# Lightning attention and a gated FFN on one core: state decay products one block ahead on POOL, crossbar transposes ahead of the output stores on SP

## Chip, core and metric

One core of a Trainium2 chip. The metric is device time in microseconds (us): the median of several executions of the same program. A profile is one further execution, recorded instruction by instruction. Engine names: PE is TensorE, DVE is VectorE, ACT is ScalarE, POOL is GpSimd; SP issues DMAs. POOL issues DMAs too.

## What is computed

Four sequences of 768 positions with eight heads of 64 (q, k, v), a decay `lam` per head, then a feed-forward layer on the 3072 x 512 result with a sigmoid gate and 1536 hidden features. The reference goes through the sequence in blocks and carries a state per head:

```
intra = (q_b k_b^T * Dmask) v_b              # Dmask[i,j] = lam^(i-j) for i >= j, else 0
inter = (q_b * lam^(pos+1)) kv_state
out_b = intra + inter
kv_state = lam^block * kv_state + (k_b * lam^(block-1-pos))^T v_b
...
y = (sigmoid(x w_gate) * (x w_val)) w_out    # x: out, as 3072 x 512
```

## The kernel before

The kernel takes blocks of 128 positions, so it has six blocks, 0 to 5, each over all four sequences (512 tokens). Matmul inputs are bf16. The heads are kept in pairs, so one 128 x 128 matmul tile holds two heads of 64.

Per block n there are these pieces; the line numbers are those of the profile of the kernel before.

- `load`: q, k, v of the block by three DMAs that POOL issues (L78, tiles qb, kb, vb; four buffers each). They convert fp32 to bf16 on the way, in packets of one head's row.
- `transpose_by_dma` (blocks 2 to 5): two crossbar transposes that SP issues (L151), first Q into QR, then K into KR. Blocks 0 and 1 are transposed on PE (L160, L169, L184, L190).
- `piece_t`: QS = QR times the powers of lam, on DVE (L177), once for each half of the sequences (two of the four).
- `piece_s`: scores sp, on PE (L206) from KR and QS. `piece_m`: MT = sp times the mask, on DVE (L214).
- `piece_a`: the attention output op, on PE from the state Sb and QS (L220) and from V and MT (L227); ACT copies it to XT (L234).
- `make_kd`: kd = K times a decay, one POOL product over 128 x 2048 (L238), two buffers.
- `piece_c`: the new state. PE makes cp from kd and V (L246). POOL makes sd = Sb times the block's decay, one product for each of the four sequences (L251, four buffers), and DVE adds the two into Sb (L259). The matmuls of the next block and the next sd read Sb.
- `piece_gv`: for one of 12 groups of 128 hidden features the gate gp (L270) and the value vp (L276), the sigmoid sg on ACT (L273) and ht = sg times vp on DVE (L279). `piece_gvh` is the same for half of the tokens.
- `piece_po`: the output po for one sequence of the block, 12 matmuls on PE (L302), a copy to ob on ACT (L305, four buffers), and a store that SP issues (L306).

PSUM has two pools: five tiles for attention (tags tq, tk, sp, op, cp) and three for the feed-forward part (gp, vp, po), given out in turn. So a gate or value matmul group waits until the ht or sg that read the tile three places earlier is through.

The order of each engine's instructions is the order in which they are written, for all of PE, POOL, DVE, ACT and SP; nothing is reordered. An engine that waits holds up everything behind it, and so does a DMA queue: SP's stores and transposes go in their written order, and so do POOL's loads and products.

In the order of before, `fetch(n)` writes the load, kd and the two transposes of a block together. `fetch(2)` stands in the middle of block 0's end, and `fetch(n+1)` at the head of block n's loop for n = 2, 3, 4. On POOL this gives, from the end of the weight loads: kd(1), load 2, kd(2), sd of block 1, load 3, kd(3), sd of block 2, load 4, kd(4), sd of block 3, load 5, kd(5), sd of block 4. On SP: the transposes of block 2, eight stores (blocks 0 and 1), transposes of block 3, four stores, transposes of block 4, four stores, transposes of block 5, eight stores.

A block of the loop (n = 2, 3, 4) runs on PE as: gate and value groups 0 and 1 with the state pieces between and behind them, groups 2 and 3 each followed by a half of QS for block n+1 (on DVE), group 4, scores of the first half, groups 5, 6, 7, scores of the second half, group 8, attention output of the first half, groups 9 to 11, attention output of the second half, then the four outputs po of block n.

Of the kernel before, what the change touches and what calls it, by code (L numbers as in the profile page):

```python
# [8 lines left out]
FP32 = mybir.dt.float32  # L9
BF16 = mybir.dt.bfloat16  # L10
AF = mybir.ActivationFunctionType
ALU = mybir.AluOpType
# [4 lines left out]
def kernel(  # L17
# [11 lines left out]
    nc = tc.nc  # L29

    B, H, S, D = q.shape
    C = 128
    NSTEP = S // C
    HP = H // 2
# [8 lines left out]
    qkv = ctx.enter_context(tc.tile_pool(name="qkv", bufs=4))  # L43
    kdp = ctx.enter_context(tc.tile_pool(name="kdp", bufs=2))
# [26 lines left out]
    def load(n, what, b0, b1):  # L71
        sl = slice(n * C, (n + 1) * C)
        for c in what:
            lst, src = {"q": (Q, q), "k": (K, k), "v": (V, v)}[c]
            if n not in lst:
                lst[n] = qkv.tile([128, B, H, D], BF16, tag=c + "b", name=c + "b")
            t = lst[n]
            nc.gpsimd.dma_start(  # L78
                out=t[:, b0:b1],
                in_=src[b0:b1, :, sl, :].rearrange("b h s d -> s (b h) d"))  # L80
# [6 lines left out]
    def load_wo(i, w):  # L87
        fs = slice(i * w, (i + 1) * w)
        nc.gpsimd.dma_start(out=WO[:, fs, :], in_=wo_r[:, fs, :])
# [35 lines left out]
    for hp in range(HP):  # L125
# [3 lines left out]
    dec = const.tile([128, HP], FP32, tag="dec")  # L129
# [4 lines left out]
                            in1=pk.rearrange("p (g u) -> p u g", u=2).unsqueeze(3).to_broadcast([128, 2, HP, C]),  # L134
                            op=ALU.mult)
# [11 lines left out]
    def transpose_by_dma(n):  # L147
        QR[n] = trsb.tile([128, B, HP, C], BF16, tag="QR", name="QR", bufs=2)
        kt = trsb.tile([128, B, HP, C], BF16, tag="KR", name="KR", bufs=2)
        for dst, src in ((QR[n], Q[n]), (kt, K[n])):  # L150
            nc.sync.dma_start_transpose(out=dst.rearrange("p b g c -> p (b g) c"),  # L151
                                        in_=src.rearrange("p b h d -> p (b h d)"))
        for bp in range(2):
            KS[n, bp] = kt[:, 2 * bp:2 * bp + 2]
# [39 lines left out]
    Sb = stp.tile([128, B, HP, 128], BF16, tag="Sb", name="Sb")  # L194
# [16 lines left out]
    def piece_m(n, b):  # L211
        MT[n, b] = mtp.tile([128, 2, HP, C], BF16, tag="MT", name="MT")
        for u in range(2):
            nc.vector.tensor_tensor(out=MT[n, b][:, u], in0=SP[n, b][u], in1=mask[:, u], op=ALU.mult)  # L214

    def piece_a(n, bs):
        for b in bs:
            OP[n, b] = ps_at.tile([128, HP, C], FP32, name="op", tag="ps")
            for hp in range(HP if n > 0 else 0):
                nc.tensor.matmul(OP[n, b][:, hp, :], lhsT=Sb[:, b, hp, :],  # L220
                                 rhs=QS[n, b // 2][:, b % 2, hp, :],
                                 start=(hp == 0), stop=False, skip_group_check=True)
        for b in bs:
            for hp in range(HP):
                for u in range(2):
                    us = slice(u * 64, (u + 1) * 64)
                    nc.tensor.matmul(OP[n, b][us, hp, :], lhsT=V[n][:, b, 2 * hp + u, :],  # L227
                                     rhs=MT[n, b][:, u, hp, :],
                                     start=(n == 0 and hp == 0), stop=(hp == HP - 1),
                                     skip_group_check=True)  # L230
        if n not in XT:
            XT[n] = xtp.tile([128, NMT, B, C], BF16, tag="XT", name="XT")
        for b in bs:
            nc.scalar.copy(XT[n][:, :, b, :], OP[n, b])  # L234

    def make_kd(n):
        KD[n] = kdp.tile([128, B, H, D], BF16, tag="kd", name="kd")
        nc.gpsimd.tensor_tensor(  # L238
            out=KD[n], in0=K[n],
            in1=kds.unsqueeze(1).unsqueeze(3).to_broadcast([128, B, H, D]), op=ALU.mult)  # L240

    def piece_c(n, bs):
        for b in bs:
            cp = ps_at.tile([128, HP, 128], FP32, name="cp", tag="ps")
            for hp in range(HP):
                nc.tensor.matmul(cp[:, hp, :], lhsT=KD[n][:, b, 2 * hp:2 * hp + 2, :],  # L246
                                 rhs=V[n][:, b, 2 * hp:2 * hp + 2, :],
                                 start=(hp == 0), stop=(hp == HP - 1), skip_group_check=True)
            if n > 0:
                sd = kdp.tile([128, HP, 128], FP32, tag="sd", name="sd", bufs=4)  # L250
                nc.gpsimd.tensor_tensor(out=sd, in0=Sb[:, b],  # L251
                                        in1=dec.unsqueeze(2).to_broadcast([128, HP, 128]),
                                        op=ALU.mult)
            for u in range(2):
                us = slice(u * 64, (u + 1) * 64)
                if n == 0:
                    nc.vector.tensor_copy(Sb[us, b, :, us], cp[us, :, us])
                else:
                    nc.vector.tensor_tensor(out=Sb[us, b, :, us], in0=cp[us, :, us],  # L259
                                            in1=sd[us, :, us], op=ALU.add)  # L260
# [4 lines left out]
    def piece_gv(n, ft):  # L265
        fs = slice(ft * 128, (ft + 1) * 128)
        x = XT[n].rearrange("p m b c -> p m (b c)")
        gp = ps_ff.tile([128, TCH], FP32, name="gp", tag="ff")
        for mt in range(NMT):
            nc.tensor.matmul(gp, lhsT=WG[:, mt, fs], rhs=x[:, mt, :],  # L270
                             start=(mt == 0), stop=(mt == NMT - 1))
        sg = htp.tile([128, TCH], BF16, tag="sg", name="sg", bufs=3)
        nc.scalar.activation(sg, gp, AF.Sigmoid)  # L273
        vp = ps_ff.tile([128, TCH], FP32, name="vp", tag="ff")
        for mt in range(NMT):
            nc.tensor.matmul(vp, lhsT=WV[:, mt, fs], rhs=x[:, mt, :],  # L276
                             start=(mt == 0), stop=(mt == NMT - 1))
        HT[n, ft] = htp.tile([128, TCH], BF16, tag="ht", name="ht", bufs=2 * NFT)
        nc.vector.tensor_mul(HT[n, ft], sg, vp)  # L279
# [19 lines left out]
    def piece_po(n, tt):  # L299
        po = ps_ff.tile([128, DM], FP32, name="po", tag="ff")  # L300
        for ft in range(NFT):
            nc.tensor.matmul(po, lhsT=HT[n, ft][:, tt * 128:(tt + 1) * 128],  # L302
                             rhs=WO[:, ft, :], start=(ft == 0), stop=(ft == NFT - 1))
        ob = osb.tile([128, DM], FP32, tag="ob", name="ob")
        nc.scalar.copy(ob, po)  # L305
        nc.sync.dma_start(out=out[tt * S + n * C:tt * S + (n + 1) * C, :], in_=ob)  # L306
# [12 lines left out]
    load(1, "v", 2, 4)  # L319
    for i in range(3):  # L320
        load_wo(i, NFT // 3)
    make_kd(1)

    idle(10)
    piece_tq0(0)
# [23 lines left out]
    def c(n, bp):  # L349
        piece_c(n, [2 * bp, 2 * bp + 1])  # L350

    def t(n, bp):
        piece_t(n, bp)

    def sc(n, bp):
        piece_s(n, [2 * bp, 2 * bp + 1])
        piece_m(n, 2 * bp)

    def m(n, bp):
        piece_m(n, 2 * bp + 1)  # L360

    def a(n, bp):
        piece_a(n, [2 * bp, 2 * bp + 1])

    def fetch(n):
        load(n, "qkv", 0, B)
        make_kd(n)
        transpose_by_dma(n)

    def gv(n, *fts):  # L370
        for ft in fts:
            piece_gv(n, ft)

    def gvh(n, i, *fts):
        for ft in fts:
            piece_gvh(n, ft, i)
# [2 lines left out]
    c(0, 0)  # L379
    gv(0, 4)  # L380
    c(0, 1)
    gv(0, 5, 6, 7)
    t(1, 0)
    gv(0, 8)
# [4 lines left out]
    a(1, 0)  # L389
    gv(0, 11)  # L390
    t(1, 1)
    fetch(2)
    gvh(1, 0, 0, 1)
    sc(1, 1)
    gvh(1, 0, 2)
# [6 lines left out]
    c(1, 0)  # L402
    gv(1, 9)
    c(1, 1)
    gv(1, 10, 11)
    piece_po(0, 0)
    t(2, 0)
# [5 lines left out]
    sc(2, 1)  # L413
    m(2, 1)
    piece_po(0, 3)
    piece_po(1, 0)
    a(2, 0)
    piece_po(1, 1)
# [3 lines left out]
    for n in range(2, NSTEP):  # L422
        nx = n + 1
        if nx < NSTEP:
            fetch(nx)
            gv(n, 0)
            c(n, 0)
            gv(n, 1)
            c(n, 1)
            gv(n, 2)  # L430
            t(nx, 0)
            gv(n, 3)
            t(nx, 1)
            gv(n, 4)
            sc(nx, 0)
            gv(n, 5)
            m(nx, 0)
            gv(n, 6, 7)
            sc(nx, 1)
            gv(n, 8)  # L440
            m(nx, 1)
            a(nx, 0)
            gv(n, 9, 10, 11)
            a(nx, 1)
        else:
            gv(n, *range(NFT))
        for tt in range(B):
            piece_po(n, tt)
# [30 lines left out]
```

## Time and profile before

| what | value |
|---|---|
| median of 4 runs (lowest, highest) | 243.15 us (242.41, 244.54) |
| profiled execution: its own time, and its span | 243.9 us, 241.7 us |
| PE busy in the span | 225.1 us (93%) |
| DVE, ACT, POOL busy | 105.6, 80.1, 85.0 us |
| mean granted TensorE clock | 0.985 |
| kd on POOL | 6 products, 3.6 us each |
| sd on POOL | 16 products, 1.09 us each |
| one load of q, k or v (blocks 2 to 5), issue to landing | 8.0, 10.3, 13.0 us (medians) |
| a transpose QR or KR, issue to landing | 7.8 or 6.2 us (medians) |

The span goes from the first to the last instruction; the own time has 2.2 us around it. A row of a timeline reads: start, duration, engine, line, operation, output<-inputs, shape, count, and in brackets the idle time before it with what ended it. SPq and POOLq are the instructions by which SP and POOL issue DMAs. In the DMA counts, q0 is the queue of the loads that POOL issues and q1 that of the stores and transposes that SP issues: packets, MB, and the time of the packets as a share of 16 engines.

### The profile page before, as it was taken

What the parts mean: (1) busy time and instruction counts of PE and PEld (TensorE: products, weight loads), DVE (VectorE), ACT (ScalarE), POOL (GpSimd) and SP (SyncE); (2) the same over time, 40 slices, a digit from 0 to 9 for tenths busy, and PEclk for the clock granted to TensorE, in tenths of its full rate; (3) what the DMA queues carried; (4) which work ended last, traced back from release to release, by engine and by line L of the source; (5) the groups of instructions that cost most, each with busy time, mean ns of one, the idle gap of its engine ahead of it and who ended that gap; (6) DMA issues with size and microseconds to landing.
All of it is one profiled execution on the core that took longest, in us unless ns stands there. A gap on an engine that the chain in (4) does not pass through costs nothing.

```text
span 241.7 us, 3816 instructions
## 1 busy us (share of the span) xinstructions
PE 225.1 (93%) x1528; PEld 116.0 (48%) x1553; DVE 105.6 (44%) x184; ACT 80.1 (33%) x145; POOL 85.0 (35%) x70
## 2 busy tenths in 40 slices
PE   7789999999999999829999999999999999999993
PEld 2444555886534555314554444554544554444441
DVE  2373855843738004455630298720397620243300
ACT  5453234453211332202431332332222432333221
POOL 8999650934962980991000085000000000000000
PEclk9999999999999999967999999999999999999999
DMA  9999999999999899999902480002560002200022
GB/s 58 137 182 195 174 183 169 206 155 157 136 112 200 169 94 180 160 155 156 81 3 87 122 140 3 0 3 87 148 115 1 0 3 87 87 0 0 3 87 87
DMA packets 102289, 24.89 MB, mean 103 GB/s; under 512 B 91520, under 2 KB 99200, under 8 KB 102272
## 3 DMA queue, kind: packets, MB, share of 16 engines
q0 software_dynamic: 82032, 14.16, 77.7%
q1 hardware_dynamic: 20240, 10.49, 19.5%
q8 instruction: 12, 0.20, 0.3%
q14 instruction: 5, 0.04, 0.0%
HBM read 28.32 MB, written 6.29 MB: 143 GB/s over the span
## 4 chain that ended last, share of the span: by engine, by line
PE 84%; DMA 6%; SPq 2%; DVE 2%; issue 2%; ACT 2%; POOL 0%; POOLq 0%; ACTq 0%; DVEq 0%
PE po L302 25%; PE vp L276 22%; PE gp L270 22%; DMA KR<-kb 4%; PE sp L206 3%; PE vp L293 3%; PE op L227 3%; DMA kb<-in_k_dram 3%; PE gp L287 2%; SPq L151 2%; PE op L220 2%; DVE MT L214 2%; PE cp L246 2%; PE tk L169 1%; ACT KS L172 0%
## 5 line engine op out<-in xcount | busy, mean ns | idle before, releaser
L279 DVE TENSOR_TENSOR ht<-sg,vp 128x512 bf16<-128x512 bf16 x65 | 44.5, 686 | 94.5 <-PE vp L276 93.2
L270 PE MATMUL gp<-XT,WG 128*128 128x512 bf16 x249 | 66.1, 383 | 1.0 <-issue 0.5
L276 PE MATMUL vp<-XT,WV 128*128 128x512 bf16 x255 | 66.8, 383 | 0.3
L273 ACT ACTIVATE sg<-gp 128x512 bf16<-128x512 f32 x65 | 38.8, 597 | 81.7 <-PE gp L270 77.6
L302 PE MATMUL po<-WO,ht 128*128 128x512 bf16 x281 | 63.3, 379 | 0.9 <-DVE ht L279 0.5
L302 PEld LDWEIGHTS <-ht 128*128 128x128 bf16 x288 | 27.6, 98 | 33.7 <-issue 0.8
L238 POOL TENSOR_TENSOR kd<-kb,kds 128x2048 bf16<-128x2048 bf16 x6 | 21.8, 3632 | 58.8 <-PE cp L246 30.2
L276 PEld LDWEIGHTS <-WV 128*128 128x128 bf16 x260 | 25.7, 99 | 31.3 <-issue 1.1
L270 PEld LDWEIGHTS <-WG 128*128 128x128 bf16 x260 | 24.2, 98 | 27.7 <-issue 2.1
L214 DVE TENSOR_TENSOR MT<-sp,mask 128x512 bf16<-128x512 f32 x48 | 30.5, 682 | 8.1 <-PE sp L206 8.1
L305 ACT COPY ob<-po 128x512 f32<-128x512 f32 x24 | 14.1, 586 | 51.4 <-PE po L302 47.7
L251 POOL TENSOR_TENSOR sd<-Sb,dec 128x512 f32<-128x512 bf16 x16 | 17.0, 1086 | 0.0
L234 ACT CAST XT<-op 128x512 bf16<-128x512 f32 x24 | 13.0, 588 | 9.9 <-PE op L227 9.8
L259 DVE TENSOR_TENSOR Sb<-cp,sd 64x256 bf16<-64x256 f32 x32 | 13.4, 420 | 1.9 <-POOL sd L251 1.0
L78 POOL DMA_DIRECT2D qb<-in_q_dram x8 | 11.9, 1484 | 1.0 <-POOLq L463 0.8
L78 POOL DMA_DIRECT2D kb<-in_k_dram x8 | 11.5, 1433 | 1.1 <-DMA qb<-in_q_dram 1.1
L78 POOL DMA_DIRECT2D vb<-in_v_dram x8 | 11.4, 1430 | 0.8 <-DMA WG<-in_moe_w_gate_dram 0.6
L206 PE MATMUL sp<-QS,KR 64*128 64x128 bf16 x128 | 5.4, 229 | 6.2 <-DMA KR<-kb 5.8
L140 PE MATMUL wm<-zero 128*128 128x512 bf16 x23 | 8.2, 489 | 1.5 <-DVE zero L97 1.2
L177 DVE TENSOR_TENSOR QS<-QR,lamq 128x1024 bf16<-128x1024 bf16 x8 | 6.4, 796 | 6.2 <-DMA QR<-qb 6.2
L206 PEld LDWEIGHTS <-KR 64*128 64x128 bf16 x128 | 3.9, 99 | 9.6 <-DMA KR<-kb 6.3
L293 PE MATMUL vp<-XT,WV 128*128 128x256 bf16 x56 | 8.4, 272 | 0.1
(51 smaller groups left out, 114.7 us busy)
## 6 DMA issues: line engine op xcount, KB each, us to landing
out_dram<-ob SPq DMA_DIRECT2D x24, 256.0 KB, 2.0
qb<-in_q_dram POOLq DMA_DIRECT2D x4, 512.0 KB, 8.0
kb<-in_k_dram POOLq DMA_DIRECT2D x4, 512.0 KB, 10.3
vb<-in_v_dram POOLq DMA_DIRECT2D x4, 512.0 KB, 13.0
WG<-in_moe_w_gate_dram POOLq DMA_DIRECT2D x6, 256.0 KB, 9.5
WV<-in_moe_w_val_dram POOLq DMA_DIRECT2D x6, 256.0 KB, 9.8
WO<-in_moe_w_out_dram POOLq DMA_DIRECT2D x3, 512.0 KB, 15.2
qb<-in_q_dram POOLq DMA_DIRECT2D x4, 256.0 KB, 7.5
```

The source lines that it names most:

```text
L78: nc.gpsimd.dma_start(out=t[:, b0:b1], in_=src[b0:b1, :, sl, :].rearrange("b h s d -> s (b h) d"))
L206: nc.tensor.matmul(sp[u][:, hp, :], lhsT=KS[n, bp][us, i, hp, :], rhs=QS[n, bp][us, i, hp, :], start=(hp == 0), stop=(hp == HP - 1), skip_ ...
L214: nc.vector.tensor_tensor(out=MT[n, b][:, u], in0=SP[n, b][u], in1=mask[:, u], op=ALU.mult)
L238: nc.gpsimd.tensor_tensor(out=KD[n], in0=K[n], in1=kds.unsqueeze(1).unsqueeze(3).to_broadcast([128, B, H, D]), op=ALU.mult)
L251: nc.gpsimd.tensor_tensor(out=sd, in0=Sb[:, b], in1=dec.unsqueeze(2).to_broadcast([128, HP, 128]), op=ALU.mult)
L270: nc.tensor.matmul(gp, lhsT=WG[:, mt, fs], rhs=x[:, mt, :], start=(mt == 0), stop=(mt == NMT - 1))
L273: nc.scalar.activation(sg, gp, AF.Sigmoid)
L276: nc.tensor.matmul(vp, lhsT=WV[:, mt, fs], rhs=x[:, mt, :], start=(mt == 0), stop=(mt == NMT - 1))
L279: nc.vector.tensor_mul(HT[n, ft], sg, vp)
L293: nc.tensor.matmul(vp[:, cs], lhsT=WV[:, mt, fs], rhs=x[:, mt, cs], start=(mt == 0), stop=(mt == NMT - 1))
L302: nc.tensor.matmul(po, lhsT=HT[n, ft][:, tt * 128:(tt + 1) * 128], rhs=WO[:, ft, :], start=(ft == 0), stop=(ft == NFT - 1))
L305: nc.scalar.copy(ob, po)
```

## The change

The sd products leave `piece_c` and become `fade()`, four products that are written right after the state update they read, one block before they are used. The loads of blocks 3 to 5 are written one loop iteration earlier (load n+2 in block n, load 3 in block 1, ahead of `fade()`), and kd follows behind `fade()`. The transposes of block 3 are written behind the fourth store of block 0 (so ahead of the four stores of block 1), those of blocks 4 and 5 ahead of the four stores of blocks 2 and 3. kd(1) moves from the weight loads to behind the first `fade()`. No instruction is added or taken away on any engine.

POOL's order from the end of the weight loads is now: sd of block 1, kd(1), load 2, kd(2), load 3, sd of block 2, kd(3), load 4, sd of block 3, kd(4), load 5, sd of block 4, kd(5). SP's: transposes of block 2, four stores, transposes of block 3, four stores, transposes of block 4, four stores, transposes of block 5, twelve stores.

```diff
+    SD = {}
+
+    def fade():
+        for b in range(B):
+            SD[b] = kdp.tile([128, HP, 128], FP32, tag="sd", name="sd", bufs=4)
+            nc.gpsimd.tensor_tensor(out=SD[b], in0=Sb[:, b],
+                                    in1=dec.unsqueeze(2).to_broadcast([128, HP, 128]),
+                                    op=ALU.mult)
+
     def piece_c(n, bs):
...
-            if n > 0:
-                sd = kdp.tile([128, HP, 128], FP32, tag="sd", name="sd", bufs=4)
-                nc.gpsimd.tensor_tensor(out=sd, in0=Sb[:, b],
-                                        in1=dec.unsqueeze(2).to_broadcast([128, HP, 128]),
-                                        op=ALU.mult)
+            sd = SD.pop(b, None)
...
-    make_kd(1)
...
-    def fetch(n):
-        load(n, "qkv", 0, B)
-        make_kd(n)
-        transpose_by_dma(n)
-
...
     c(0, 1)
+    fade()
+    make_kd(1)
     gv(0, 5, 6, 7)
...
     t(1, 1)
-    fetch(2)
+    load(2, "qkv", 0, B)
+    make_kd(2)
+    transpose_by_dma(2)
...
     c(1, 1)
+    load(3, "qkv", 0, B)
+    fade()
+    make_kd(3)
     gv(1, 10, 11)
...
     piece_po(0, 3)
+    transpose_by_dma(3)
     piece_po(1, 0)
...
     for n in range(2, NSTEP):
         nx = n + 1
         if nx < NSTEP:
-            fetch(nx)
             gv(n, 0)
             c(n, 0)
             gv(n, 1)
             c(n, 1)
+            if n + 2 < NSTEP:
+                load(n + 2, "qkv", 0, B)
+                fade()
+                make_kd(n + 2)
+            elif nx < NSTEP - 1:
+                fade()
...
             m(nx, 1)
+            if n + 2 < NSTEP:
+                transpose_by_dma(n + 2)
             a(nx, 0)
```

## The prediction

> Times are us from the start of the span in the profiled execution unless said otherwise; block n is 128 positions of every sequence, sp(n,h) the scores of its half h.
>
> **What bounds the kernel now.** First the page: who is busy, and where the TensorE clock dips.
>
> ```profile
> span 241.7 us, 3816 instructions
> ...
> PE 225.1 (93%) x1528; PEld 116.0 (48%) x1553; DVE 105.6 (44%) x184; ACT 80.1 (33%) x145; POOL 85.0 (35%) x70
> ...
> PEclk9999999999999999967999999999999999999999
> ```
>
> PE is the bound; a change can only win in its 16.6 us of idle time and where its clock is low. One place has both, so next the waits of PE and the chain of waits there:
>
> ```profile
> PE sp L206 <- DMA KR<-kb: 5.8, 1, 5.8
> ```
>
> ```profile
> 92.84 0.33 SPq L306
> ...
> 93.26 5.57 SPq L151
> ...
> 98.92 8.47 DMA KR<-kb
> ...
> 107.44 1.03 PE sp L206 x16
> 108.48 1.82 PE gp L270 x4
> ```
>
> The pair of transposes of block 3 (Q, then K) stands on SP behind the eighth output store, so it is issued at 93.26, although its input was there at 77 (its kd started at 77.21). K lands at 107.4; sp(3,0) had nothing else to wait for from 101.67. The table of stretches shows what comes after the stall (ninth column: granted clock):
>
> ```profile
> 102.00:104.00 2.00, 0.00 (x0) 0.00 (x0) 0.00 (x0) 0.00 (x0) 2.00 (x3) 1.00 1.35 134
> 106.00:108.00 2.00, 0.56 (x12) 0.56 (x14) 2.00 (x4) 0.00 (x0) 2.00 (x2) 0.50 0.76 118
> 108.00:110.00 2.00, 2.00 (x14) 0.80 (x9) 1.42 (x3) 0.00 (x0) 1.83 (x2) 0.50 2.28 146
> ```
>
> The clock falls to half some 2.8 us into the idle time and is back near 111.8. The whole price is read from the starts of blocks 2, 3 and 4, which do the same PE work:
>
> ```profile
> 91.98 1.03 PE L270 MATMUL gp<-XT,WG 128*128 128x512 bf16 x4
> 135.39 1.03 PE L270 MATMUL gp<-XT,WG 128*128 128x512 bf16 x4
> 170.93 1.03 PE L270 MATMUL gp<-XT,WG 128*128 128x512 bf16 x4
> ```
>
> Block 2 takes 43.41, block 3 35.54: the stall costs 7.87, of it 5.77 idle and 2.10 slow clock.
>
> **Part 1, transposes ahead of the stores (-7.87).** All eight crossbar transposes remain; three pairs move up on SP. Block 3's pair now stands behind store 4 (issued 80.19) and is ready to go near 79.6, once part 2's gain is taken off. Under load traffic the pair took 14.1 from first issue to landing (93.26 to 107.4), so at worst it lands near 93.7; sp(3,0) wants it at 101.67 - 0.96 = 100.7. Cover 7 us: the stall and its clock go whole. Queued behind it on SP are stores 5 to 8, late by up to 11.7 (5.57 + 6.14 of issue). That costs nothing: a store frees one of four ob tiles, next written by block 2's outputs after 118. The pairs of blocks 4 and 5 move past four stores each; before, they were issued at 136.64 and 172.17 and nobody waited; now they go as soon as their loads land. Behind the stall nothing else is late: sp(3,1) and all after it follow at PE's own pace.
>
> The skill's page "TensorE: Matmul & The Clock Gate" (Part 1) gives one window of about 3.4 us at half speed after an idle window; by that the slow clock would cost 1.7 and the sum of this part 7.5, against the trace's 7.87.
>
> **Part 2, state decay one block ahead (-0.96).** The same 16 sd (17.0 us of POOL) and 6 kd (21.8), in another order. Before, block 1's sd stood behind kd(2), which waited for its load: POOL kd 57.69, sd 61.27, and the state add waited 1.02 for it (62.33 instead of 61.31). The add delayed the ht behind it, and these the matmul groups that need their PSUM tiles: the matmuls of the preceding group end their issue at 64.70 and 66.70, the next start at 64.98 and 67.38, together 0.28 + 0.68 = 0.96. Now sd(1) runs after the last WO issue (34.54), 4.1 us long, ahead of kd(1), which waits for its K until 41.73 in any case: free. Later blocks showed no wait for sd, so they win nothing. Bounds 0 to 0.96; I take 0.96, since the waiting ht are in the rows.
>
> **Part 3, loads earlier (0, bounds 0 to +9.9).** Load 3 is issued behind kd(2) at 61.3, not behind sd(1) at 65.25; its first packets follow 2.6 later (as 65.25 to 67.8), at 63.9. The K transpose of block 2 moved its data from 64.4 to 66.0 on an empty DMA; now it shares. What sharing does is seen in the DMA counts between 99 and 100, where load 4 and block 3's Q transpose ran together:
>
> ```profile
> q0 software_dynamic: 412, 0.05, 79.8%
> q1 hardware_dynamic: 411, 0.11, 79.6%
> ```
>
> One to one; a load alone does about 1235 packets per us, and a transpose has some 2080. So K of block 2 lands near 64.4 + 2080/411 + 0.4 = 69.9 (no sharing: 66.4); sp(2,0) wants it at 72.66 - 0.96 = 71.7. Free, with 1.8 to spare. Load 3 loses 5 us x (1 - 412/1235) = 3.3 and lands its K at 77.1 - 3.95 + 3.3 = 76.5, so kd(3) starts then.
>
> **Part 4, what POOL now does beside DVE (+2.9, bounds 0 to +5.4).** kd now stands behind sd, hence behind the state adds, and falls on the two QS products of L177 (both inputs in SBUF). The trace has this meeting once, in block 3:
>
> ```profile
> 139.99 3.61 POOL L238 TENSOR_TENSOR kd<-kb,kds 128x2048 bf16<-128x2048 bf16 x1 [30.17 <-PE cp L246]
> 143.58 1.48 POOL L251 TENSOR_TENSOR sd<-Sb,dec 128x512 f32<-128x512 bf16 x1
> ```
>
> ```profile
> 142.82 1.34 DVE L177 TENSOR_TENSOR QS<-QR,lamq 128x1024 bf16<-128x1024 bf16 x1
> 144.08 0.68 DVE L279 TENSOR_TENSOR ht<-sg,vp 128x512 bf16<-128x512 bf16 x1
> 144.68 0.92 DVE L177 TENSOR_TENSOR QS<-QR,lamq 128x1024 bf16<-128x1024 bf16 x1
> ```
>
> A free QS takes 0.68. This one began 0.78 before kd's end and ended 0.56 after it: next to nothing was done beside kd. And sd, 1.03 when free, took 1.48 around the QS. I read it as: one stands until the other is through, and the one that waits goes next. ht and MT, with one input in PSUM, kept their 0.68 beside POOL.
>
> The skill's "SBUF — State Buffer" (Who interferes with whom) speaks against the change here: a VectorE instruction with two SBUF inputs and a GpSimd instruction that reads SBUF exclude each other for the whole instruction. By the rule the cost is the 2.9 worked out below, by the row's bare +0.66 it is nothing.
>
> Block 3, in the times of before: adds end 142.18, last sd 142.35 to 143.4; QS(0) comes at 142.82 and goes next, to 143.9; kd(5) then until about 147.5; QS(1), due at 144.5, ends 147.5 + 0.56 = 148.05; the ht behind it at 148.65. The gate group whose PSUM tile that ht frees (ps_ff has three) started at 147.31, now 148.7: +1.4 on PE, and 0.05 more at the next. Block 2 is alike if load 4's K is there by 99: kd(3) ends 80.1, load 4's first packets come 2.6 later at 82.7, load 3 needed 9.3 from there to K's landing (67.8 to 77.1), sharing with block 3's K transpose adds 3.3 and two more stores 0.9 each (one took the load from 2470 to 1348 packets between 74 and 76): 97. So 2 x 1.45. Lower end 0 (the +0.66 reading, or a K later than QS(1)); upper 2 x 2.7 (kd ahead of QS(0), so that sp at 145.02 waits until 147.7). kd(3) at 76.5 misses QS(2,1), due at 75.49 - 0.96 = 74.5.
>
> **Sum.** -7.87 - 0.96 + 2.90 = -5.93. The profiled execution's own time was 243.9 (span 241.7 and 2.2 around it): 238.0 against it. It lies 0.75 above the median of the runs shown, 243.15, so for the median 237.2.
>
> **Rivals.**
> A. The new meetings on POOL and DVE cost PE nothing (K of block 4 too late, or QS merely slowed): 243.15 - 8.83 = 234.3. For: DVE is busy 44%. Against: the 1.34 row, and kd(5)'s place.
> B. Block 2 gets a wait: kd(3) starts by 74.5 because load 3 lost less than 3.3, and holds QS(2,1). If it starts at 73.2 (77.1 - 3.95), it ends 76.8, QS 77.4, sp(2,1) 2.1 late: 239.3; at 74.5, 3.4 late: 240.6. Against: it needs K's transpose not to have slowed load 3.
> C. The order on SP changes but block 3's pair still lands after 100.7, held by load 4: then only part 2 is left, 242.2. Against: it would need 21 us instead of 14.1.
> D. Slower: block 2's K transpose gets no share while load 3 runs. Load 3 has 12288 packets, from 63.9 at 1235 per us until 73.9, stores 1 and 2 make it 76.5; then 2080 packets at 800 per us (as at 105 to 107) and 0.4: lands 79.5, sp(2,0) 7.8 late, and 2.1 of slow clock: -5.93 + 9.9 = +4.0, 247.1. For: the Q transposes issued at 53.92 and 93.26 showed their first packets only at 58.5 and 98.5, both under a load. Against: the 1:1 counts, and that K's packets flow at 64.4, before load 3's. It decides from a landing at 75.5 (3.8 + 2.1 = 5.9).
>
> **How the numbers follow.** Chances: forecast 0.48, A 0.26, B 0.14, C 0.05, D 0.07. About 1%, 2.4 us, is what a measurement can tell from no change: faster means below 240.7. Forecast, A and nearly all of B lie there (0.86); C, B's upper end with a slow clock and the milder D within 1% (0.09); D from a landing at 78 on is slower (0.05). The range leaves out C and D and takes in A and B, with 0.5 around: 233.8 to 241.0.
>
> **What would show it.** Right: no wait of sp for KR in PE's waits; PEclk 9 all through from the second slice; block 2's length 35.5 to 37; the first state add of block 1 without a wait for sd; QS of blocks 3 and 4 of over 2 us each beside kd, and a gate group 1.4 late for ht. Wrong: sp(2,0) waiting for KR near 72 (D), QS(2,1) long near 74.5 (B), QS at 0.68 everywhere (A). The forecast fails if load 3's K, or load 4's, lands some 2 us from where I put it.

## The result, and the profile after

| kernel | median, us | runs | lowest to highest |
|---|---|---|---|
| before | 243.48 | 63 | 242.15 to 244.62 |
| changed | 242.85 | 44 | 238.03 to 244.23 |

The ratio is 0.9894, 95% interval 0.9875 to 0.9913. It is formed over the runs within 1.5% of each kernel's fastest, which for the changed kernel are ten of 44, all with a mean granted clock of 0.996 or more, while over all runs the medians are 0.3% apart. So the change brought between 0.6 and 2.6 us, where 5.9 was forecast and 237.2 expected. The profiled execution of the changed kernel took 244.07, 1.2 above its median. The wide spread of the changed kernel goes for the most part with the granted clock (section "Both remedies").

The page of the changed kernel, the lines that answer to those shown of before:

```profile
span 242.3 us, 3816 instructions
...
PE 226.2 (93%) x1528; PEld 116.3 (48%) x1553; DVE 114.8 (47%) x184; ACT 80.1 (33%) x145; POOL 85.6 (35%) x70
...
PEclk9999999999999599999999999999999999999999
```

The dip of the clock is still there, but it has moved from slices 18 and 19 to slice 14. PE's waits say what is waited for now (total, times, longest):

```profile
PE sp L206 <- DVE QS L177: 3.6, 1, 3.6
PE gp L275 <- DVE ht L284: 2.4, 2, 1.2
```

The wait for KR is gone; one of sp for QS has come, and two for ht. The chain of waits around sp(2,1), which runs between the outputs of block 0, and the two instructions on POOL and DVE at that time:

```profile
73.03 1.88 DVE MT L214 x3
74.90 3.94 DVE QS L177
...
78.89 1.04 PE sp L206 x16
79.93 7.83 PE po L307 x24
```

```profile
74.67 3.62 POOL L238 TENSOR_TENSOR kd<-kb,kds 128x2048 bf16<-128x2048 bf16 x1 [3.21 <-DMA kb<-in_k_dram]
```

```profile
74.82 4.01 DVE L177 TENSOR_TENSOR QS<-QR,lamq 128x1024 bf16<-128x1024 bf16 x1
```

kd(3) starts 0.15 us ahead of QS(2,1). QS(2,1), 0.68 us of work, ends 0.54 after kd(3) has ended. In the kernel before the two did not meet (POOL, DVE, PE):

```profile
77.21 3.62 POOL L238 TENSOR_TENSOR kd<-kb,kds 128x2048 bf16<-128x2048 bf16 x1 [6.85 <-DMA kb<-in_k_dram]
```

```profile
75.49 0.68 DVE L177 TENSOR_TENSOR QS<-QR,lamq 128x1024 bf16<-128x1024 bf16 x1
```

```profile
76.23 0.62 PE L206 MATMUL sp<-QS,KR 64*128 64x128 bf16 x16 [0.26 <-DVE QS L177]
```

The table of stretches (ninth column: granted clock) shows the second half of the price:

```profile
76.00:78.00 2.00, 0.00 (x0) 0.00 (x0) 2.00 (x1) 0.00 (x0) 2.00 (x1) 1.00 2.04 242
78.00:80.00 2.00, 1.11 (x17) 0.90 (x18) 1.30 (x2) 0.00 (x0) 2.00 (x3) 0.55 0.35 132
80.00:82.00 2.00, 2.00 (x6) 0.64 (x5) 2.00 (x4) 0.00 (x0) 2.00 (x2) 0.50 0.90 57
82.00:84.00 2.00, 2.00 (x6) 0.73 (x5) 0.02 (x1) 0.00 (x0) 1.33 (x1) 0.50 2.44 158
84.00:86.00 2.00, 2.00 (x8) 0.84 (x7) 0.00 (x0) 0.59 (x1) 0.00 (x0) 0.74 2.54 155
```

PE stands until 78.9 and then runs at half clock until about 85. The starts of blocks 2 to 5:

```profile
97.60 1.03 PE L275 MATMUL gp<-XT,WG 128*128 128x512 bf16 x4
...
134.56 1.03 PE L275 MATMUL gp<-XT,WG 128*128 128x512 bf16 x4
...
171.53 1.03 PE L275 MATMUL gp<-XT,WG 128*128 128x512 bf16 x4
...
207.06 1.03 PE L275 MATMUL gp<-XT,WG 128*128 128x512 bf16 x4
```

Block 2 took 43.41 and takes 36.96; block 3 took 35.54 and takes 36.97; block 4 stays at 35.53. What holds blocks 2 and 3 by some 1.43 each is seen in block 2:

```profile
105.62 4.07 POOL L238 TENSOR_TENSOR kd<-kb,kds 128x2048 bf16<-128x2048 bf16 x1
```

```profile
106.73 3.50 DVE L177 TENSOR_TENSOR QS<-QR,lamq 128x1024 bf16<-128x1024 bf16 x1
110.16 0.67 DVE L284 TENSOR_TENSOR ht<-sg,vp 128x512 bf16<-128x512 bf16 x1
```

```profile
110.88 1.02 PE L275 MATMUL gp<-XT,WG 128*128 128x512 bf16 x4 [1.21 <-DVE ht L284]
```

kd(4) holds QS(3,1), the ht behind it is late, and a gate group waits for the PSUM tile that this ht frees.

Where the time went, from the starts in both timelines (the first gate group of block 0 at 17.48 before and 17.77 after; the first po at 67.38 and 66.71; sp(2,1) at 76.23 and 78.89; block 2 at 91.98 and 97.60):

| stretch | before | after | difference | forecast |
|---|---|---|---|---|
| up to block 0's first gate group | 17.48 | 17.77 | +0.29 | 0 |
| from there to the first po (sd earlier) | 49.90 | 48.94 | -0.96 | -0.96 |
| first po to sp(2,1) (QS(2,1) held) | 8.85 | 12.18 | +3.33 | 0 |
| sp(2,1) to block 2 (half clock) | 15.75 | 18.71 | +2.96 | 0 |
| block 2: stall gone, QS(3,1) held | 43.41 | 36.96 | -7.87 + 1.42 | -7.87 + 1.45 |
| block 3: QS(4,1) held | 35.54 | 36.97 | +1.43 | +1.45 |
| sum (spans 241.7 and 242.3) | | | +0.6 | -5.9 |

This is the account of two executions. The 2.96 of half clock is the dearer of two sizes that the runs show (last section).

### The profile page after: what moved, and what is told of

Same layout as the page of the kernel before. It is cut to its first block, busy times and chain, and to the rows that moved or that the text cites. A ratio compares the mean times of both kernels' runs of the same rounds, so it can differ in the third digit from the quotient of the medians.

```text
span 242.3 us, 3816 instructions
## 1 busy us (share of the span) xinstructions
PE 226.2 (93%) x1528; PEld 116.3 (48%) x1553; DVE 114.8 (47%) x184; ACT 80.1 (33%) x145; POOL 85.6 (35%) x70
## 3 DMA queue, kind: packets, MB, share of 16 engines
q0 software_dynamic: 82032, 14.16, 79.6%
## 4 chain that ended last, share of the span: by engine, by line
PE 87%; DVE 4%; DMA 3%; issue 2%; POOL 2%; ACT 1%; POOLq 0%; DVEq 0%
PE po L307 26%; PE gp L275 23%; PE vp L281 23%; DMA kb<-in_k_dram 3%; PE sp L206 3%; PE vp L298 3%; PE op L227 3%; PE gp L292 2%; PE cp L255 2%; PE op L220 2%; DVE MT L214 2%; DVE QS L177 2%; POOL qb L78 1%; DVE ht L284 1%; POOL kb L78 0%
## 5 line engine op out<-in xcount | busy, mean ns | idle before, releaser
L275 PE MATMUL gp<-XT,WG 128*128 128x512 bf16 x249 | 65.2, 379 | 3.3 <-DVE ht L284 2.4
L281 PE MATMUL vp<-XT,WV 128*128 128x512 bf16 x255 | 66.0, 379 | 0.3
L307 PE MATMUL po<-WO,ht 128*128 128x512 bf16 x281 | 65.9, 390 | 0.4
L307 PEld LDWEIGHTS <-ht 128*128 128x128 bf16 x288 | 28.3, 100 | 35.0 <-issue 3.5
L238 POOL TENSOR_TENSOR kd<-kb,kds 128x2048 bf16<-128x2048 bf16 x6 | 22.7, 3784 | 13.5 <-PE gp L275 8.1
L177 DVE TENSOR_TENSOR QS<-QR,lamq 128x1024 bf16<-128x1024 bf16 x8 | 15.8, 1969 | 0.0
L302 DVE TENSOR_TENSOR ht<-sg,vp 128x256 bf16<-128x256 bf16 x14 | 5.8, 419 | 6.1 <-PE vp L298 3.8
## 6 DMA issues: line engine op xcount, KB each, us to landing
WV<-in_moe_w_val_dram POOLq DMA_DIRECT2D x6, 256.0 KB, 10.6
```

The costliest lines, as they stand in the source:

```text
L177: nc.vector.tensor_tensor(out=QS[n, bp], in0=QR[n][:, 2 * bp:2 * bp + 2], in1=lamq.unsqueeze(1).to_broadcast([128, 2, HP, C]), op=ALU.mult)
L238: nc.gpsimd.tensor_tensor(out=KD[n], in0=K[n], in1=kds.unsqueeze(1).unsqueeze(3).to_broadcast([128, B, H, D]), op=ALU.mult)
L275: nc.tensor.matmul(gp, lhsT=WG[:, mt, fs], rhs=x[:, mt, :], start=(mt == 0), stop=(mt == NMT - 1))
L281: nc.tensor.matmul(vp, lhsT=WV[:, mt, fs], rhs=x[:, mt, :], start=(mt == 0), stop=(mt == NMT - 1))
```

## The experiments

Theory 1 is the reading above: a QS product (two inputs in SBUF) and a POOL product that reads SBUF shut each other out for a whole instruction, the waiting one goes next, and kd now meets QS three times. Theory 2: POOL's volume merely slows QS, as a shared rate. Theory 3: the loss is a late landing, of load 3 or of a transpose pushed ahead on SP.

| run | median, us | ratio to before (95% interval) | blocks 2, 3, 4, us |
|---|---|---|---|
| before | 243.5 | | 43.41, 35.54, 35.53 |
| changed | 242.85 | 0.9894 (0.9875 to 0.9913) | 36.96, 36.97, 35.53 |
| kd in four | 236.07 | 0.9708 (0.9678 to 0.9737) | 35.53, 35.53, 35.54 |
| load 3 behind sd | 236.83 | 0.9724 (0.9703 to 0.9744) | 35.53, 36.97, 35.54 (second run) |
| no kd(5) | 241.27 | 0.9899 (0.9871 to 0.9928) | 36.97, 35.53, 35.54 |
| block 3's pair alone | 237.76 | 0.9782 (0.9753 to 0.9811) | 37.27, 35.53, 35.54 |
| POOL's part alone | 242.74 | 0.9952 (0.9917 to 0.9988) | 36.97, 36.97, 35.54 |
| kd in four, load 3 behind sd | 235.41 | 0.9661 (0.9632 to 0.9691) | 35.53, 35.53, 35.54 |
| added product, block 4 | 236.88 (one) | | 35.53, 35.53, 37.16 |
| added fills, block 4 | 235.66 (one) | | block 4: 35.54 |

### kd as four products

```diff
-        nc.gpsimd.tensor_tensor(
-            out=KD[n], in0=K[n],
-            in1=kds.unsqueeze(1).unsqueeze(3).to_broadcast([128, B, H, D]), op=ALU.mult)
+        for b in range(B):
+            nc.gpsimd.tensor_tensor(
+                out=KD[n][:, b], in0=K[n][:, b],
+                in1=kds.unsqueeze(2).to_broadcast([128, H, D]), op=ALU.mult)
```

> The changed kernel with each kd product written as four products of 128 x 512, one for each sequence; everything else stays. Theory 1 (a QS product and a POOL product shut each other out for one instruction, and the waiting one goes next): a held QS waits for one quarter, about 0.93 us, not for 3.6; QS(2,1) ends in time for sp(2,1) or at most 0.9 late, no slow clock, blocks 2 and 3 take about 35.6 us instead of 36.97. Time near 243.5 - 7.87 - 0.96 = 234.7, at most 235.7. Theory 2 (it is the volume of POOL's work beside DVE that slows QS, shared as a rate): kd still takes 3.6 in all and QS is as long as before, time near 242.8. Theory 3 (the loss is a late landing of load 3 or of a transpose): nothing changes, 242.8.

Measured: 236.07, 6.8 us below the changed kernel with the same work, order and transfers. POOL and DVE in block 3:

```profile
135.70 4.94 POOL L239 TENSOR_TENSOR kd<-kb,kds 128x512 bf16<-128x512 bf16 x4
```

```profile
135.10 1.18 DVE L177 TENSOR_TENSOR QS<-QR,lamq 128x1024 bf16<-128x1024 bf16 x1
...
136.81 0.93 DVE L177 TENSOR_TENSOR QS<-QR,lamq 128x1024 bf16<-128x1024 bf16 x1
```

kd takes longer in all (4.94, and 4.04 when nothing meets it, against 3.61), yet QS(4,1) goes from 3.50 to 0.93. That is not a shared rate, and no landing was moved (kd(3) still starts when its K lands, at 74.75): theories 2 and 3 fail for these meetings. A piece of kd(3) still met QS(2,1) in this profile (QS 1.48, sp(2,1) waited 1.05 where before it was 0.26), without a slow clock. The time lies 0.4 above the upper end expected, though that end had allowed for a wait of up to 0.9. In the profile 0.79 of the span is this wait, and 0.32 is a later start of block 0's first gate group (17.80, before 17.48), which the estimate did not hold.

### Load 3 behind the sd products

```diff
-    load(3, "qkv", 0, B)
     fade()
+    load(3, "qkv", 0, B)
     make_kd(3)
```

> The changed kernel with load 3 written behind the first sd products of block 1's end, where POOL issued it before; everything else stays. Theory 1: kd(3) then starts some 4 us later than 74.67, near 77 to 78.7, behind QS(2,1) at 74.8; QS(2,1) takes 0.7, the 3.3 us of wait and 2.96 us of slow clock in block 2 are gone, blocks 2 and 3 stay at 36.97. Time near 242.85 - 6.3 = 236.6. Theory 3 (landings): a later load 3 can only make block 2 worse, 243 or more.

> A second look at the changed kernel with load 3 behind the sd products, for its profile. Theory 1: kd(3) starts behind the start of QS(2,1); QS(2,1) takes 0.68, no wait of sp(2,1) above 0.3, no slow clock in block 2, blocks 2 and 3 take 36.97 each.

Measured: 236.83, the median of five. Four of them took 236.48 to 236.95; the first, which was the profiled one, took 598.75, with the 512-column matmuls of PE at 0.83 us each instead of 0.38, for a reason that stays open. A second run, for a profile, took 236.61. Its POOL and DVE lines around QS(2,1):

```profile
79.54 3.61 POOL L238 TENSOR_TENSOR kd<-kb,kds 128x2048 bf16<-128x2048 bf16 x1 [7.52 <-DMA kb<-in_k_dram]
```

```profile
74.83 0.68 DVE L177 TENSOR_TENSOR QS<-QR,lamq 128x1024 bf16<-128x1024 bf16 x1
```

A later load makes the kernel 6 us faster: kd(3) comes after QS(2,1), and the whole price of that stall (3.33 + 2.96 = 6.3) is gone. Against theory 3, as it was put. One expectation failed: block 2 took 35.53 here, not 36.97. The K of load 4 landed so late that kd(4) started only at 103.20, behind QS(3,1) at 100.45. So that meeting, too, hangs on a landing. The spans of the two profiles, 242.3 and 234.6, differ by 7.7, which is 6.3 and the 1.43 of block 2; the medians differ by only 6.0. So the expected 236.6 came true partly by luck: 1.43 more was won, and the changed kernel's median lies 1.2 below the profiled execution from which the 6.3 was read.

### Without kd(5)

Left out is kd(5), which nothing reads.

```diff
-                make_kd(n + 2)
+                if n + 2 < NSTEP - 1:
+                    make_kd(n + 2)
```

> The changed kernel without the product kd(5), which nothing reads (the state after the last block is not needed), so the output is the same. Theory 1: QS(4,1) takes about 0.7 to 0.9 instead of 3.50, block 3 takes 35.5 instead of 36.97, block 2 stays at 36.96; time 1.4 less than the changed kernel, about 241.4. Theory 2: about the same saving if the rate of kd is what slows QS. Theory 3: no change, 242.8.

Measured: 241.27, and block 3 at 35.53 with QS(4,1) back at its bare length, while block 2, whose kd(4) stayed, took 36.97:

```profile
104.82 3.50 DVE L177 TENSOR_TENSOR QS<-QR,lamq 128x1024 bf16<-128x1024 bf16 x1
...
141.79 0.68 DVE L177 TENSOR_TENSOR QS<-QR,lamq 128x1024 bf16<-128x1024 bf16 x1
```

A product whose output nobody reads cost 1.44 us of PE's time, since it held QS(4,1).

### The two halves of the change, each alone

Block 3's pair ahead of the stores of block 1, POOL as before:

```diff
     piece_po(0, 3)
+    transpose_by_dma(3)
     piece_po(1, 0)
...
-            fetch(nx)
+            if nx > 3:
+                fetch(nx)
```

(load 3 and kd(3) are written behind `c(1, 1)`, the same place in POOL's order)

> The kernel before with one thing changed: the two transposes of block 3 are written behind the fourth store, ahead of the four stores of block 1; POOL keeps its order of before (load 3 and kd(3) are written earlier in the text for that, in the same place of POOL's order). Theory 1: the stall and its slow clock go (7.87), and block 2 is held only if kd(4), which started at 97.16, is still running when QS(3,0) comes at 99.4: between 0 and 2.7 us. Time 243.5 - 7.87 = 235.6 to 238.3. If the move on SP were itself the loss (its transposes colliding with load 4): 242 or more.

And POOL's part with SP's order as before:

```diff
-    transpose_by_dma(3)
...
         if nx < NSTEP:
+            transpose_by_dma(nx)
             gv(n, 0)
...
-            if n + 2 < NSTEP:
-                transpose_by_dma(n + 2)
             a(nx, 0)
```

> The other half alone: sd one block ahead, loads and kd as in the changed kernel, but all transposes on SP where they were before (block 3's pair behind the eighth store, those of blocks 4 and 5 at the head of the next block). Theory 1: QS(2,1) is held by kd(3) as in the changed kernel (+3.3 and up to 3 of slow clock), block 3's pair is issued near 98 when load 4 is almost through, lands some 7 to 9 us later, and sp(3,0), due 107, waits 0 to 1; in blocks 2 and 3 QS(,1) is held as before (1.4 each). Time 242.5 to 245, within 1% of the kernel before and of the changed one. If the earlier transposes were what cost the changed kernel its gain: 237 or less.

Measured: 237.76 and 242.74. Block 3's pair moved up on SP alone gives 2.2%. In that run kd(4) meets QS(3,0), the first QS product in block 2, instead; POOL, DVE and PE:

```profile
99.81 3.61 POOL L238 TENSOR_TENSOR kd<-kb,kds 128x2048 bf16<-128x2048 bf16 x1 [10.02 <-DMA kb<-in_k_dram]
```

```profile
100.18 3.79 DVE L177 TENSOR_TENSOR QS<-QR,lamq 128x1024 bf16<-128x1024 bf16 x1
```

```profile
104.12 0.62 PE L206 MATMUL sp<-QS,KR 64*128 64x128 bf16 x16 [1.67 <-DVE QS L177]
```

POOL's part alone has all three meetings, and in it block 3's pair, though still behind eight stores, was not waited for:

```profile
98.34 2.08 SPq L151 DMA_TRANSPOSE QR<-qb  x1
100.52 3.55 SPq L151 DMA_TRANSPOSE KR<-kb  x1
```

```profile
74.84 3.51 DVE L177 TENSOR_TENSOR QS<-QR,lamq 128x1024 bf16<-128x1024 bf16 x1
```

The stall of sp(2,1) makes all later work on PE late, load 4 is through by then, the pair is issued in 2.08 and 3.55 us instead of 5.57 and 6.14, and sp(3,0) at 106.68 has no wait. With POOL in this order the move on SP therefore gives nothing that the medians show: 242.74 without it, 242.85 with it. The gains of the halves do not add.

### A product, and fills, added where none were

Both start from kd in four. Block 4 has no kd and no sd behind its state adds (the `elif` branch that goes is never taken). Added there is a product that reads Sb, or (second edit) a tiny product that reads Sb and two fills; nothing reads their output.

```diff
-            elif nx < NSTEP - 1:
-                fade()
+            else:
+                dead = kdp.tile([128, B, H, D], BF16, tag="kd", name="dead")
+                nc.gpsimd.tensor_tensor(
+                    out=dead, in0=Sb.rearrange("p b g (u d) -> p b (g u) d", d=D),
+                    in1=kds.unsqueeze(1).unsqueeze(3).to_broadcast([128, B, H, D]), op=ALU.mult)
```

```diff
-            elif nx < NSTEP - 1:
-                fade()
+            else:
+                tick = kdp.tile([128, B], FP32, tag="tick", name="tick")
+                nc.gpsimd.tensor_tensor(out=tick, in0=Sb[:, :, HP - 1, 127], in1=dec, op=ALU.mult)
+                dead = kdp.tile([128, B, H, D], BF16, tag="kd", name="dead")
+                for i in range(2):
+                    nc.gpsimd.memset(dead, float(i))
```

> The changed kernel with kd in four, and in block 4, which has no kd and no sd behind its state adds, one added POOL product of 128 x 2048 that reads Sb (so it starts behind the last add) and whose output nothing reads. Theory 1: it starts some 0.6 us ahead of QS(5,0) and holds it for its 3.6 us; QS(5,0) takes about 3.6 instead of 0.68, sp(5,0) waits about 1.4, block 4 takes 36.95 instead of 35.54, blocks 2 and 3 stay at 35.5. Theory 2 (shared rate): QS(5,0) at most about 1.4. Theory 3: nothing changes in block 4.

> As the run with the added product in block 4, but the added POOL work there only writes: a product of 128 x 4 that reads Sb (so that the rest starts behind the last state add), then two fills of 128 x 2048, whose output nothing reads. If POOL and a QS product shut each other out whenever POOL is busy, QS(5,0) is again held, up to the end of the fill it meets, and block 4 takes over 36 us. If it is the reading of SBUF by both that shuts them out, QS(5,0) takes 0.68 beside the fill, sp(5,0) has no wait, and block 4 takes 35.5 us.

Measured with the product (POOL, DVE, PE):

```profile
169.21 3.62 POOL L443 TENSOR_TENSOR dead<-Sb,kds 128x2048 bf16<-128x2048 bf16 x1 [29.50 <-DVE Sb L265]
```

```profile
169.70 3.67 DVE L177 TENSOR_TENSOR QS<-QR,lamq 128x1024 bf16<-128x1024 bf16 x1
```

```profile
173.52 0.62 PE L206 MATMUL sp<-QS,KR 64*128 64x128 bf16 x16 [1.56 <-DVE QS L177]
```

and with the fills (POOL, DVE):

```profile
169.75 3.67 POOL L446 MEMSET dead<- 128x2048 bf16 x2
```

```profile
170.18 0.68 DVE L177 TENSOR_TENSOR QS<-QR,lamq 128x1024 bf16<-128x1024 bf16 x1
```

The same time of POOL work (one product of 3.62, or two fills of 3.67 together) holds QS for 3 us when it reads SBUF, and not at all when it only writes. So it is not POOL's being busy, nor its writes. This is as the Trainium skill has it in "SBUF — State Buffer" (Who interferes with whom): a VectorE instruction with two SBUF inputs contends with a GpSimd instruction that reads SBUF, not with one that only writes it, and the first one has the port for its whole instruction.

### Both remedies

kd in four and load 3 behind sd.

> The changed kernel with both edits: kd as four products of 128 x 512, and load 3 behind the sd products of block 1's end. Theory 1: kd(3) no longer meets QS(2,1), so the 1.05 us that sp(2,1) still waited with kd in four goes down to the 0.26 of the kernel before; blocks 2, 3 and 4 take 35.5 us each, no slow clock. Span about 234.0 - 0.8 = 233.2, time about 235.2, at or just below the time with kd in four alone (236.07). Theory 3 (the landing of load 3 matters in itself): slower than with kd in four alone.

Measured: 235.41 (235.15 to 235.54), ratio 0.9661: faster than both kernels, and at the median than either remedy alone (236.07 and 236.83; the runs with kd in four, 235.41 to 237.60, overlap with these). Blocks 2, 3 and 4 take 35.5 each, and sp(2,1) is back at the wait it had before the change:

```profile
75.88 0.62 PE L206 MATMUL sp<-QS,KR 64*128 64x128 bf16 x16 [0.25 <-DVE QS L177]
```

Its spread is 0.4 us over six runs, that of the changed kernel 6.2 over 44. The mean granted clock on record for each execution sorts these 44:

| mean granted clock | executions | time, us | median |
|---|---|---|---|
| 0.996 to 0.999 | 11 | 238.03 to 241.62 | 241.13 |
| 0.989 to 0.992 | 24 | 242.10 to 243.65 | 242.86 |
| 0.983 to 0.985 | 9 | 243.17 to 244.23 | 243.75 |

So the spread goes with the clock for the most part. The profiled execution is of the last group, and all of its slow clock lies behind the stall of sp(2,1); its 244.07 less the 2.96 of half clock is 241.11, the median of the first group. That QS(2,1) was held in nearly all 44, and that they differ in what this stall cost in clock, is therefore likely, but argued, not shown, since only one was profiled. Only the fastest lies further off: 2.8 below the next, about what a QS(2,1) that gets through would win (3.3). In the profile kd(3) starts just 0.15 us ahead of QS(2,1).

## Why the prediction was wrong

**Part 1, the transposes: right in size, with another cover.** The stall of block 3 and its clock are gone (with kd in four block 2 takes 35.53, 7.88 less than before), and nobody waits for the stores behind the pair. One reading of before was off, without effect on the sum: the clock fell to half near 104.9, 3.2 us into the idle time, not 2.8. The pair, though, was issued at 86.19, not at 79.6, since the fourth store, ahead of it on SP, came behind the stall of sp(2,1) and its slow clock, at 85.81:

```profile
86.19 6.40 SPq L151 DMA_TRANSPOSE QR<-qb  x1
92.70 4.37 SPq L151 DMA_TRANSPOSE KR<-kb  x1
```

K landed 6.4 after its issue, at 99.1; sp(3,0) ran at 107.22.

**Part 2, sd earlier: right,** -0.96 as worked out, and the state add's wait for sd (1.0 before) is gone from DVE's waits.

**Part 3, the loads: here it failed.** The step was "Load 3 loses 5 us x (1 - 412/1235) = 3.3 and lands its K at 77.1 - 3.95 + 3.3 = 76.5, so kd(3) starts then", and with it, in part 4, that kd(3) misses QS(2,1). The K of load 3 landed 10.6 after its issue, at 74.2, and kd(3) started at 74.67:

```profile
61.84 1.74 POOL L78 DMA_DIRECT2D qb<-in_q_dram  x1
63.57 1.70 POOL L78 DMA_DIRECT2D kb<-in_k_dram  x1
```

The counts from 65 to 66 and from 66 to 67 show why:

```profile
q1 hardware_dynamic: 1135, 0.29, 127.7%
```

```profile
q0 software_dynamic: 1011, 0.13, 202.1%
q1 hardware_dynamic: 206, 0.05, 23.2%
```

The K transpose of block 2 had the DMA engines to itself until 66, and load 3 followed alone, at some 1230 packets per us: the two hardly shared. Load 3 was issued at 61.84 and showed its first packets 4.3 us later, not 2.6. A wait costs it about 1.7 us, a share would have cost 3.3. The row of 1 to 1 counts was right for what it showed, and it comes back where load 4 meets block 3's pair (from 92 to 93):

```profile
q1 hardware_dynamic: 406, 0.10, 82.0%
q0 software_dynamic: 409, 0.05, 79.7%
```

It was carried to a pair of transfers that stood otherwise: here the transpose was under way when the load began. That this is the reason is not shown. Besides, the 77.1 of before held one store in front of load 3's K; in the changed kernel store 1's packets came at 74, when that K was through. The wait in place of the share is 1.6 us less, the store 0.9 by the prediction's own price, and load 3 was issued 0.54 later than the 61.3 of the estimate. Together that is the 2 us by which the estimate was late (76.5 against a landing at 74.2 and a start of kd(3) at 74.67). The margin between kd(3) and QS(2,1) had been put at 2.0, so the error was of the size that decides.

**The rival that came true is B,** but at its upper end, and dearer than it was priced. It had QS(2,1) 2.1 to 3.4 late and named a slow clock behind that end without adding it. Measured: 3.33 and 2.96 of clock, 6.3 in all. B with this clock would have ended at 237.2 + 6.3 = 243.5, above the range of 233.8 to 241.0 (the measured median is 242.85); leaving the clock out of B's price made the range too narrow, and 0.14 was too little for a meeting with 2 us to spare at a place where every landing moves.

**Part 4, POOL beside DVE: right.** 2 x 1.45 was forecast, 1.42 and 1.43 measured, by the way described: QS(·,1) held, ht late, a gate group waiting for its PSUM tile. The upper bound of 2.7, for kd ahead of QS(·,0), was too high: the two places that showed it cost 1.7 (block 3's pair alone) and 1.6 (the added product).

Rivals A, C and D did not come: no QS product in blocks 2 and 3 ran free, block 3's pair was in time, and K of block 2 landed at 69.5. The 69.9 forecast for it was met by luck. It rested on 5 us of even sharing; instead all but 32 of the transpose's packets had gone by 66.2, and these 32 came between 68 and 69, beside load 3. In D's price the two stores, at the 0.9 each that part 4 counts, lead from 73.9 to 75.7 and not to 76.5; nothing hangs on it.

## What to carry to other kernels

Before moving work on POOL, list where DVE runs an instruction with two SBUF inputs, and compare starts: one long POOL product that reads SBUF and begins just ahead of it holds the whole DVE queue for its length (3.5 to 4.0 us here instead of 0.68), whatever the busy shares say. Cutting the product into short instructions bounds the hold for little (one kd takes 4.04 us on POOL instead of 3.61, and the kernel 6.8 less). And price a rival with everything that follows it: the stalls of PE seen here that were 3.1 to 5.8 us long cost 1.3 to 3.0 us more in lowered clock, while one of 1.05 us (kd in four) cost none.

## What was not expected of the hardware

- The price of the clock after a stall differs for stalls of one kind. From sp(2,1) to block 2 is 15.75 us at full clock. After 3.59 us of idle time it took 18.71 in the changed kernel, after 3.08 in POOL's part alone 18.66, but after 3.14 in the run without kd(5) only 17.08: 2.96, 2.91 and 1.33 more. The tables of stretches show the difference. The clock reads 0.50 inside a slow stretch and 1.00 outside, so a row of 2 us with mean m holds 4 x (1 - m) us at half clock. POOL's part alone (the three rows between these two read 0.50), then the run without kd(5):

```profile
76.00:78.00 2.00, 0.00 (x0) 0.00 (x0) 2.00 (x1) 0.00 (x0) 2.00 (x2) 0.90 1.70 297
...
84.00:86.00 2.00, 2.00 (x10) 0.86 (x9) 0.00 (x0) 0.58 (x1) 0.00 (x0) 0.89 2.57 156
```

```profile
78.00:80.00 2.00, 1.39 (x18) 0.92 (x19) 1.30 (x3) 0.00 (x0) 2.00 (x3) 0.51 0.22 82
80.00:82.00 2.00, 2.00 (x7) 0.78 (x6) 1.74 (x3) 0.00 (x0) 2.00 (x2) 0.63 1.21 84
```

  That is 6.8 us at half clock in POOL's part alone and 3.4 without kd(5). The changed kernel has 6.8, and so has the kernel before (rows of 0.73, 0.50, 0.50 and 0.56 from 104 to 112), twice the one window that the prediction's estimate of 1.7 took. The Trainium skill's "TensorE: Matmul & The Clock Gate" (Part 1) has a free-running window of about 3.4 us, which would let the price depend on when the stall falls; no run here moved a stall against the window, so that is not shown. The measured stretches are as long as one and two such windows.
- Load 3's first packets came 4.3 us after its issue while a transpose was in flight, load 4's 2.6 us after its own (issue at 78.23, packets from 80.9). Why the first one waited, and why transposes and loads share in one place and not in the other, stays open.
